# Window attention with a convolutional position term: moving two 64 by 64 matmul stages next to each other, pairing the layer norm's transposes, and reordering the setup and the last block

## The chip, the core and the metric

One NeuronCore of a Trainium2 chip runs the whole program. The metric is device time in microseconds (us) of one execution; the time before is the median of two runs, 5380.8 us (5376.48 and 5385.11). The engines: TensorE (PE in the profile; its weight loads are PEld), VectorE (DVE), ScalarE (ACT), GpSimd (POOL), and SyncE (SP), whose queue here issues nearly all DMAs. PSUM is the memory that TensorE writes; GpSimd has no part in reading it here, so whatever GpSimd adds is first copied to SBUF by ScalarE.

## The reference

```python
# x: (1, 511, 511, 192) bf16; ws = 7, nh = 4, dh = 48
pe = sum over 3x3 taps of shifted x * dw_pe[i, j]      # depthwise convolution
x0 = x + pe
h  = (x0 - mean) / sqrt(var + 1e-5)                    # over the 192 channels
hw = h cut into 73 x 73 windows of 49 tokens
q, k, v = split(hw @ w_qkv)                            # 4 heads of 48
out = softmax(q k^T * 48**-0.5) v @ w_o
return x0 + out                                        # windows put back
```

## The kernel before

**Tiling.** The 5329 windows are cut into 42 blocks: 41 of 128 windows and one of 81. In a block the 128 partitions are windows. `X` (three buffers in turn) holds the block as windows x 49 tokens x 192 channels, `XP` the 9 x 9 patch of every window as 81 partitions x 128 windows x channels, `T` the convolution (with the residual's own tap left to a separate add) as an 81 x 49 matrix for each channel. `HO` (two buffers) holds the normalised tokens channels-first (two halves `kt` of 96 channels); the attention's result is written back into it.

**A group** is 8 windows of a block (16 groups in a block, 11 in the last, 667 in all). Iteration g of the main loop (line 544) issues, in this order on TensorE: q of group g (`stage_A` which=0, line 364); the transposes of the attention result of group g-2 (`stage_E`, 447); k of group g (`stage_A` which=1); the product of probabilities and v of group g-1 (`stage_D`, 423); projections of the block before (`proj`, 459; 13 in a block, 4 tokens each, in groups 2 to 10); one set of layer norm transposes of the next block (`ln_tr`, 343; 7 sets in a block, in groups 10 to 15); the scores (`stage_B`, 402); v (`stage_V`, 380). B and D consist of 32 matmuls each, which use the array as four tiles of 64 by 64 (`tile_position`); all other stages use up to 128 rows and more than 64 columns. `q_`, `k_`, `v_`, `pt` and `o_` are single buffers.

**PSUM.** Every stage takes the next of three two-bank tiles `PS` in turn (`self.PS.next()`), so the fourth stage after one waits until that one's result has been read out. ScalarE reads q, k, v, the exponential of the scores, the projections and the second transpose half; VectorE reads D (a reciprocal and a multiply, lines 432 and 433), the first transpose half, and E in the first groups of a block (ScalarE later, `late`). The convolution has two one-bank tiles `PC`.

**What fills in.** The 192 convolution matmuls of the next block (`conv_mm`, line 298, one per channel, 81 x 128 weights and 49 columns; every ten a VectorE cast into `X`, line 303) are handed out by `fill()` between the long matmuls of `stage_A`, `stage_V` and `proj`, in equal shares for each long matmul, over the first 7 groups of a block. After that `hook(share)`, called at fixed places of an iteration, issues the next block's layer norm in program order: `xs` loads on SP, adds and statistics on VectorE (310, 314), `rstd` and the normalisation on GpSimd (320, 321, 329), then `XP` loads for the block after and the stores on SP. The order on every queue is the program's (`tc.manual_schedule()`); each engine runs its queue in order.

**A transpose set** (`ln_tr`) issues 8 matmuls for `kt` 0, the VectorE copy of that half, 8 matmuls for `kt` 1 and the ScalarE copy, all on one `PS` tile:

```python
            for kt in range(2):
                for i in range(N):
                    mm(pb[0:KT, kt * 1024 + i * 128 : ...], ..., is_transpose=True)
                eng = nc.vector.tensor_copy if kt == 0 else nc.scalar.copy
                eng(out=HO[b % 2][0:KT, kt, :, s0 : s0 + N], in_=pb[0:KT, kt * 1024 : ...])
```

**Setup and ends.** `__init__` clears the buffers, builds `T` in 25 tiles of two tokens (lines 120 and 129), folds the weights and reads a flag that chooses between `fast` and `slow`; `fast` runs. It then loads `XP` of block 0, convolves, normalises and transposes it with nothing beside it (lines 528 to 541), and only then enters the main loop. After the last group, one iteration does all 13 projections of the last block: matmuls, ScalarE copy (`pO`, two buffers), GpSimd add (467), stores on SP.

Of the kernel before, what the change touches and what calls it, by code (L numbers as in the profile page):

```python
# [9 lines left out]
BF = mybir.dt.bfloat16  # L10
# [3 lines left out]
ALU = mybir.AluOpType  # L14
# [47 lines left out]
class _Kernel:  # L62
    def __init__(self, ctx, tc, x, dw_pe, w_qkv, w_o, out, eps, logit_lim):
# [9 lines left out]
        self.PC = _Rot([psum.tile([128, 512], F32, name=f"psc{i}") for i in range(2)])  # L73
        for t in self.PS.t + self.PC.t:
            nc.vector.memset(t[:], 0.0)

        self.ident = consts.tile([128, 128], BF, name="ident")
        make_identity(nc, self.ident[:])
        self.zero = consts.tile([16, C], BF, name="zero")
        nc.vector.memset(self.zero[:], 0.0)  # L80
        self.XP = big.tile([128, BLK, C], BF, name="XP")
        self.XPr = self.XP[0:KP].rearrange("(r q) n c -> q r n c", q=9)
        self.T = big.tile([128, C, S], BF, name="T")
# [4 lines left out]
        gi = consts.tile([1, 1], I32, name="gi")  # L88
        nc.vector.memset(self.XP[:], 0.0)
        for t in self.X:  # L90
            nc.gpsimd.memset(t[:], 0.0)

        with tc.tile_pool(name="setup", bufs=1) as setup:
# [3 lines left out]
            for j in range(3):  # L97
                nc.sync.dma_start(out=dwK[9 * j : 9 * j + 3, :], in_=dw_pe[j])
            for kt in range(2):
# [15 lines left out]
            )  # L115
            for n, s0 in enumerate(range(0, S, 2)):
                ns = min(2, S - s0)
                ps = self.PS.next()
                for ss in range(ns):
                    nc.tensor.matmul(  # L120
                        ps[0:KP, ss * C : (ss + 1) * C],
                        lhsT=Sel[0:21, (s0 + ss) * KP : (s0 + ss + 1) * KP],
                        rhs=dwK[0:21, :],
                        start=True,
                        stop=True,
                    )
                dst = self.T[0:KP, :, s0 : s0 + ns].rearrange("p c s -> p s c")
                src = ps[0:KP, 0 : ns * C].rearrange("p (s c) -> p s c", c=C)
                (nc.vector.tensor_copy if n % 2 == 0 else nc.scalar.copy)(out=dst, in_=src)
# [43 lines left out]
            nc.vector.tensor_copy(out=gi[:], in_=gm[:])  # L173

        cond = nc.values_load(gi[0:1, 0:1], min_val=0, max_val=1)
        with tc.If(cond > 0) as cnd:
            with ExitStack() as c2, tc.manual_schedule():
                self.fast(c2)
        with cnd.Else():
            with ExitStack() as c2:  # L180
                self.slow(c2)


    def fast(self, ctx):
# [38 lines left out]

        def dram(t, h, w, dims):
            return bass.AP(tensor=t.tensor, offset=t.offset + (h * W + w) * C, ap=[list(d) for d in dims])

        zero = self.zero[0:9, :]

        def clear(part, p0, n):

            return lambda: nc.sync.dma_start(
                out=part[:, p0 : p0 + n, :], in_=bass.AP(tensor=zero.tensor, offset=zero.offset, ap=[list(zero.ap[0]), [0, n], [1, C]])
            )

        def load_xp(b):

            for a0, b0, da, db, n, p0 in blocks[b]:
                left = [0] if b0 == 0 else []
                right = [] if b0 + (n - 1) * db < NWC - 1 else list(range(n)) if da else [n - 1]
                if left and any(ln[1] for bb in blocks[:b] for ln in bb):  # L240
                    yield clear(XPr[0], p0, n if da else 1)
                if right and b:
                    yield clear(XPr[8], p0 + right[0], len(right))
                last = a0 + (n - 1) * da
                cuts = [0] + ([1] if da and a0 == 0 else []) + ([n - 1] if da and last == NWR - 1 else []) + [n]
                for i, j in zip(cuts, cuts[1:]):
                    if j <= i:
                        continue
                    top, bot = a0 + i * da == 0, a0 + (j - 1) * da == NWR - 1
                    if top and b:  # L250
                        yield clear(XP[0:9], p0 + i, j - i)
                    if bot and b:
                        yield clear(XP[KP - 9 : KP], p0 + i, j - i)
                    pr0, pr1 = (1 if top else 0), (8 if bot else 9)
                    for pc in range(9):
                        q, sh = (WS - 1, -1) if pc == 0 else (0, 1) if pc == 8 else (pc - 1, 0)
                        n0, n1 = i, j
                        if pc == 0 and left:
                            n0 = j if da else i + 1
                        if pc == 8 and right:  # L260
                            n1 = i if da else j - 1
                        if n1 <= n0:
                            continue
                        dims = [[W * C, pr1 - pr0], [WS * C * (W * da + db), n1 - n0], [1, C]]
                        dst = XPr[pc, pr0:pr1, p0 + n0 : p0 + n1, :]
                        src = dram(x, WS * (a0 + n0 * da) - 1 + pr0, WS * (b0 + n0 * db + sh) + q, dims)
                        yield lambda dst=dst, src=src: nc.sync.dma_start(out=dst, in_=src)

# [56 lines left out]

        def ln_norm(b, s0, s1):
            assert b < 2 or stored.get(b - 2, 0) * 2 * WS >= s1 or stored.get(b - 2, 0) == len(CHUNKS)
            i, n = (49 if s0 == S - 1 else s0), s1 - s0
            nc.gpsimd.tensor_tensor(  # L329
                out=hbuf(b)[:, s0:s1, :],  # L330
                in0=self.X[b % 3][:, s0:s1, :],
                in1=rstd[:, i : i + n].unsqueeze(2).to_broadcast([128, n, C]),
                op=ALU.mult,
            )

        def ln_tr(b, s0, n):
            h = hbuf(b)
            ps = PS.next()
            pb = ps[:].bitcast(BF)
            N = min(8, S - s0)  # L340
            for kt in range(2):
                for i in range(N):
                    mm(  # L343
                        pb[0:KT, kt * 1024 + i * 128 : kt * 1024 + (i + 1) * 128],
                        lhsT=h[:, s0 + i, kt * KT : (kt + 1) * KT],
                        rhs=ident[:],
                        start=True,
                        stop=True,
                        is_transpose=True,
                    )  # L350
                eng = nc.vector.tensor_copy if kt == 0 else nc.scalar.copy
                eng(  # L352
                    out=HO[b % 2][0:KT, kt, :, s0 : s0 + N],
                    in_=pb[0:KT, kt * 1024 : kt * 1024 + N * 128].rearrange("p (s w) -> p w s", w=128),
                )
# [3 lines left out]
        def stage_A(b, ck, which, fill):  # L359
            dst = (q_, k_)[which]  # L360
            ps = PS.next()
            for ab in range(2):
                for kt in range(2):
# [6 lines left out]
                    )  # L370
                    fill()
            nc.scalar.copy(out=dst[:, :, 0:TOK], in_=two_bank(ps, TOK))  # L372

        def stage_V(b, ck, fill, eng):
            ps = PS.next()
            for pi in range(4):
                w = ck * CH + 2 * pi
                col = (pi // 2) * 512 + (pi % 2) * C
                for kt in range(2):
# [6 lines left out]
                    )  # L386
                    fill()
            eng(  # L388
# [83 lines left out]
        def stat_items(b):  # L472
# [54 lines left out]

        xp = list(load_xp(0))
        for t in xp:
            t()  # L530
        n = Next(0)
# [12 lines left out]
        for g in range(NG + LE + 1):  # L544
# [100 lines left out]
    def slow(self, ctx):  # L645
# [22 lines left out]
        for t in (v_, pt):  # L668
            nc.vector.memset(t[:], 1.0)
        mm = nc.tensor.matmul  # L670

        def two_bank(ps, ncol):
# [213 lines left out]
```

## Time and profile before

| | |
|---|---|
| median of two runs | 5380.8 us (5376.48 to 5385.11) |
| the profiled execution | 5363.58 us; its span 5361.9 us |
| mean granted TensorE clock | 0.777 of full |
| PE busy, PE weight loads busy | 4426.2 us (83%), 3610.8 us (67%) |
| ACT, DVE, POOL busy | 3054.3 us (57%), 2727.6 us (51%), 2116.4 us (39%) |
| DMA | 377 MB, mean 70 GB/s |

The span is the time from the first to the last instruction; the profiled execution has 1.7 us around it. [...] Matmuls are pipelined and overlap in the records, so a busy share of PE is not its share of the peak; the waits before instructions and the start of one stage to the start of the next say more.

### The profile page before, as it was taken

The page shows a single profiled execution, that of the slowest core. Times are in us where ns is not written, and L with a number is a line of the kernel's source. Part 1 is how long each engine was busy: PE and PEld are TensorE (multiplying, and loading weights), DVE is VectorE, ACT ScalarE, POOL GpSimd, SP SyncE. Part 2 cuts the span into 40 slices and gives each one's busy share as a digit, 9 for nine tenths or more (in the row PEclk, how much of TensorE's full clock was granted, in tenths as well). Part 3 has the DMA queues.
Part 4 walks back from the last instruction along what each step waited for, and adds up shares of the span by engine and source line. Part 5 has one row for each costly group of instructions (what it writes and reads, how often), then busy time and mean ns, then how long its engine had stood idle before and what let it go on. Part 6 is the DMA issues. An engine that isn't in the chain of part 4 may idle for free. (4 is left out here: it accounts for less than half of the span.)

```text
span 5361.9 us, 167300 instructions
## 1 busy us (share of the span) xinstructions
PE 4426.2 (83%) x75049; PEld 3610.8 (67%) x75049; DVE 2727.6 (51%) x4190; ACT 3054.3 (57%) x3855; POOL 2116.4 (39%) x1188
## 2 busy tenths in 40 slices
PE   2688888888888888888888888888888888888777
PEld 1566776776766666677766766666667776676665
DVE  5554555455555544555545555545554555455542
ACT  1455555556555565556655555555555566555555
POOL 3433333334444433334433444433333343344333
PEclk9886787777777776778877777767777888777777
DMA  2222222233333222222323333222222233233221
GB/s 69 59 68 67 68 68 68 68 78 77 82 80 83 72 68 68 68 68 68 78 68 77 83 80 83 71 67 68 68 68 68 68 78 73 70 74 81 68 48 32
DMA packets 529706, 377.00 MB, mean 70 GB/s; under 512 B 454181, under 2 KB 454373, under 8 KB 528979
## 3 DMA queue, kind: packets, MB, share of 16 engines
q1 hardware_dynamic: 528531, 365.92, 27.9%
q8 instruction: 589, 9.65, 0.8%
q14 instruction: 138, 1.13, 0.1%
q10 hardware_dynamic: 448, 0.30, 0.0%
HBM read 265.31 MB, written 100.27 MB: 68 GB/s over the span
## 5 line engine op out<-in xcount | busy, mean ns | idle before, releaser
L467 POOL TENSOR_TENSOR X<-X,pO 128x768 bf16<-128x768 bf16 (+1 forms) x546 | 894.6, 1654 | 2789.2 <-ACT pO L463 2787.9
L364 PE MATMUL ps<-HO,Wqk 96*128 96x392 bf16 x5336 | 1639.4, 426 | 20.1 <-ACT HO L352 15.8
L298 PEld LDWEIGHTS <-XP 81*128 81x128 bf16 x8064 | 1246.8, 185 | 139.2 <-issue 51.6
L298 PE MATMUL psc<-T,XP 81*128 81x49 bf16 x8064 | 1303.1, 211 | 41.3 <-DMA xs<-in_x_dram 32.0
L380 PE MATMUL ps<-Wv,HO 96*128 96x192 bf16 x5336 | 863.4, 299 | 118.3 <-DVE o L433 112.2
L343 PE MATMUL ps<-ident,X 128*96 128x128 bf16 x4116 | 412.0, 253 | 640.9 <-DVE HO L352 592.0
L432 DVE RECIPROCAL rs<-ps 128x16 f32<-128x16 f32 x667 | 169.8, 255 | 1393.8 <-PE ps L423 896.8
L303 DVE CAST X<-psc 128x490 bf16<-128x490 f32 x840 | 542.8, 646 | 591.5 <-PE psc L298 585.0
L364 PEld LDWEIGHTS <-Wqk 96*128 96x128 bf16 x5336 | 623.7, 124 | 303.8 <-issue 238.1
L352 ACT COPY HO<-ps 96x1024 bf16<-96x1024 bf16 (+1 forms) x294 | 284.5, 968 | 869.7 <-PE ps L343 869.7
L343 PEld LDWEIGHTS <-X 128*96 128x96 bf16 x4116 | 336.8, 148 | 644.7 <-issue 598.6
L372 ACT CAST k<-ps 128x784 bf16<-128x784 f32 x667 | 543.6, 815 | 363.8 <-PE ps L364 269.6
L329 POOL TENSOR_TENSOR X<-X,rstd 128x1536 bf16<-128x1536 bf16 (+1 forms) x294 | 734.2, 2515 | 18.5 <-DMA out_dram<-X 5.4
L380 PEld LDWEIGHTS <-HO 96*128 96x128 bf16 x5336 | 604.6, 122 | 158.6 <-issue 111.7
L459 PE MATMUL ps<-Wo,HO 96*128 96x192 bf16 x4116 | 690.6, 302 | 16.3 <-ACT HO L448 12.7
L388 ACT CAST v<-ps 128x768 bf16<-128x768 f32 x667 | 535.7, 803 | 267.3 <-PE ps L380 218.7
L372 ACT CAST q<-ps 128x784 bf16<-128x784 f32 x667 | 543.7, 815 | 249.2 <-PE ps L364 240.9
L433 DVE TENSOR_TENSOR o<-ps,rs 128x768 bf16<-128x768 f32 x667 | 638.4, 957 | 23.4
L459 PEld LDWEIGHTS <-HO 96*128 96x128 bf16 x4116 | 619.1, 180 | 25.2 <-issue 3.5
L463 ACT CAST pO<-ps 128x768 bf16<-128x768 f32 x504 | 401.4, 799 | 392.3 <-PE ps L459 333.4
L447 PEld LDWEIGHTS <-o 128*96 128x96 bf16 x5336 | 526.4, 166 | 104.5 <-issue 45.8
L410 ACT ACTIVATE pt<-ps 128x784 bf16<-128x784 f32 x667 | 550.8, 826 | 62.6 <-PE ps L402 62.5
(55 smaller groups left out, 4068.3 us busy)
## 6 DMA issues: line engine op xcount, KB each, us to landing
XP<-in_x_dram SPq DMA_DIRECT2D x568, 216.0 KB
xs<-in_x_dram SPq DMA_DIRECT2D x574, 168.0 KB
out_dram<-X SPq DMA_DIRECT2D x246, 336.0 KB
XP<-in_x_dram SPq DMA_DIRECT2D x151, 212.6 KB
out_dram<-X SPq DMA_DIRECT2D x82, 168.0 KB
XP<-in_x_dram SPq DMA_DIRECT2D x16, 192.0 KB
XP<-in_x_dram SPq DMA_DIRECT2D x64, 30.4 KB
xs<-in_x_dram SPq DMA_DIRECT2D x63, 23.6 KB
```

The costliest lines, as they stand in the source:

```text
L298: mm(cv.ps[:, (c % 10) * S : (c % 10 + 1) * S], lhsT=XP[0:KP, :, c], rhs=T[0:KP, c, :], start=True, stop=True)
L303: nc.vector.tensor_copy(out=self.X[cv.b % 3][:, :, c0 : c0 + n], in_=cv.ps[:, 0 : n * S].rearrange("p (c s) -> p s c", s=S))
L329: nc.gpsimd.tensor_tensor(out=hbuf(b)[:, s0:s1, :], in0=self.X[b % 3][:, s0:s1, :], in1=rstd[:, i : i + n].unsqueeze(2).to_broadcast([128, ...
L343: mm(pb[0:KT, kt * 1024 + i * 128 : kt * 1024 + (i + 1) * 128], lhsT=h[:, s0 + i, kt * KT : (kt + 1) * KT], rhs=ident[:], start=True, stop ...
L364: mm(ps[:, ab * 512 : ab * 512 + TOK], lhsT=self.Wqk[kt][0:KT, which * 2 + ab, :], rhs=HO[b % 2][0:KT, kt, ck * CH : (ck + 1) * CH, 0:S], ...
L372: nc.scalar.copy(out=dst[:, :, 0:TOK], in_=two_bank(ps, TOK))
L380: mm(ps[:, col : col + C], lhsT=HO[b % 2][0:KT, kt, w : w + 2, :].rearrange("p w s -> p (w s)"), rhs=self.Wv[kt][0:KT, :], start=(kt == 0) ...
L388: eng(out=v_[:].rearrange("p (b j) h e -> p b (j h) e", b=2)[:, :, :, 0:DH], in_=two_bank(ps, 2 * C).rearrange("p b (g d) -> p b g d", d=DH),)
L410: nc.scalar.activation(out=pt[:, 0 : 16 * S].rearrange("p (b n) -> p b n", b=2), in_=two_bank(ps, 8 * S), func=ACTF.Exp, scale=SCALE)
L433: nc.vector.tensor_tensor(out=o_[:].rearrange("p b q (h d) -> p b (q h) d", d=DH), in0=ov[:, :, :, 0:DH], in1=r_[:].rearrange("p (b g) -> ...
L459: mm(ps[:, col : col + C], lhsT=HO[b % 2][0:KT, kt, :, s0 + i], rhs=self.Wo[kt][0:KT, :], start=(kt == 0), stop=(kt == 1))
L467: nc.gpsimd.tensor_tensor(out=xv, in0=xv, in1=o[:, 0:n, :], op=ALU.add)
```

## The change

- **Adjacent stages.** `stage_D` moves from before the projections and transposes to just before `stage_B`, so that the 64 by 64 stages follow each other.
- **Paired transposes.** `ln_tr` issues all 16 transposes of a set, then the two copies.
- **Convolution.** `proj` calls `fill()` no more; `stage_A` calls it with weight 2 and `stage_V` with weight 1 for each matmul (24 in all).
- **First block.** Three of the seven normalisations of block 0 go to VectorE.
- **Last block.** Seven of the 13 projections of the last block (`direct`) are added by VectorE straight from PSUM, without ScalarE and GpSimd.
- **Setup.** `T` is built in 13 tiles of four tokens, cast with another order of elements; `XP` is cleared first, by VectorE and GpSimd; `X` is cleared last; the `dw_pe` loads go to ScalarE's queue; the loads of `XP` for block 0 (`load_xp`, moved out of `fast` unchanged, with `clear` and `dram`) are issued before the flag is read.

```diff
-        for t in self.PS.t + self.PC.t:
-            nc.vector.memset(t[:], 0.0)
+        self.XP = big.tile([128, BLK, C], BF, name="XP")
+        nc.vector.memset(self.XP[:, 0:88, :], 0.0)
+        nc.gpsimd.memset(self.XP[:, 88:BLK, :], 0.0)
...
-        nc.vector.memset(self.XP[:], 0.0)
-        for t in self.X:
-            nc.gpsimd.memset(t[:], 0.0)
...
-                nc.sync.dma_start(out=dwK[9 * j : 9 * j + 3, :], in_=dw_pe[j])
+                nc.scalar.dma_start(out=dwK[9 * j : 9 * j + 3, :], in_=dw_pe[j])
...
-            for n, s0 in enumerate(range(0, S, 2)):
-                ns = min(2, S - s0)
+            make_identity(nc, self.ident[:])
+            for t in self.PS.t + self.PC.t:
+                nc.vector.memset(t[:], 0.0)
+            for n, s0 in enumerate(range(0, S, 4)):
+                ns = min(4, S - s0)
...
+                if ns == 4:
+                    dst = self.T[0:KP, :, s0 : s0 + ns].rearrange("p c (b s) -> p c b s", b=2)
+                    src = ps[0:KP].rearrange("p (b n) -> p b n", b=2)[:, :, 0 : 2 * C].rearrange("p b (s c) -> p c b s", c=C)
...
+            for t in self.X:
+                nc.gpsimd.memset(t[:], 0.0)
+        for t in self.load_xp(0):
+            t()
         cond = nc.values_load(gi[0:1, 0:1], min_val=0, max_val=1)
...
-        def ln_norm(b, s0, s1):
+        def ln_norm(b, s0, s1, eng=nc.gpsimd):
...
-            nc.gpsimd.tensor_tensor(
+            eng.tensor_tensor(
...
                         is_transpose=True,
                     )
+            for kt in range(2):
                 eng = nc.vector.tensor_copy if kt == 0 else nc.scalar.copy
...
-                    fill()
+                    fill(2)
...
-                    fill()
+                    fill(1)
...
-        def proj(b, s0, fill):
+        def proj(b, s0, direct=False):
...
-                    fill()
+            if direct:
+                for i0 in range(0, n, 2):
+                    m = min(2, n - i0)
+                    xv = self.X[b % 3][:, s0 + i0 : s0 + i0 + m, :]
+                    nc.vector.tensor_tensor(
+                        out=xv, in0=ps[:, i0 * 256 : i0 * 256 + m * C].rearrange("p (s c) -> p s c", c=C), in1=xv, op=ALU.add
+                    )
+                return
...
-                            items.append((2, lambda s0=s0: ln_norm(b, s0, min(S, s0 + 8))))
+                            items.append((2, lambda s0=s0: ln_norm(b, s0, min(S, s0 + 8), nc.vector if b == 0 and s0 % 16 else nc.gpsimd)))
...
-            nlong = 16 + 8 * len(pj)
...
-            def fill():
-                quota[0] += (conv_goal - conv_start) / nlong
+            def fill(weight):
+                quota[0] += (conv_goal - conv_start) * weight / 24
...
-            if 0 <= g - LD < NG:
-                stage_D()
             for s0 in pj:
-                proj(b - 1, s0, fill)
+                proj(b - 1, s0, b == NB and s0 % 8 == 0)
...
             hook(0.55)
             now[0] = g + 0.5
+            if n and g < NG:
+                n.transpose(part(0.56, 0.96, 7), 0.9)
+            if 0 <= g - LD < NG:
+                stage_D()
             if g < NG:
-                if n:
-                    n.transpose(part(0.56, 0.96, 7), 0.9)
                 stage_B()
```

## Rows read from the trace of the kernel before

**Rows 1.** Waits of PE: what for, us in total, times, longest us.
```profile
PE ps L343 <- DVE HO L352: 592.0, 294, 8.8
```

**Rows 2.** Timeline of one late group: start us, us, instructions [idle before <- releaser].
```profile
2621.03 0.61 PE L343 MATMUL ps<-ident,X 128*96 128x128 bf16 x8 [0.23 <-ACT HO L448]
2621.21 0.96 DVE L433 TENSOR_TENSOR o<-ps,rs 128x768 bf16<-128x768 f32 x1
2622.08 1.21 DVE L352 COPY HO<-ps 96x1024 bf16<-96x1024 bf16 x1
2623.34 0.61 PE L343 MATMUL ps<-ident,X 128*96 128x128 bf16 x8 [1.71 <-DVE HO L352]
2623.88 0.44 PE L402 MATMUL ps<-q,k 48*64 48x49 bf16 x32
2624.26 0.83 PE L380 MATMUL ps<-Wv,HO 96*128 96x192 bf16 x8
```

**Rows 3.** Windows, three blocks: stretch, us, busy by engine (count), granted clock, DMA.
```profile
2018.10:2150.60 132.50, 114.91 (x1798) 92.02 (x1797) 63.36 (x99) 72.91 (x92) 49.11 (x28) 0.68 0.28 68
2150.60:2273.40 122.80, 105.06 (x1798) 86.05 (x1797) 64.37 (x99) 72.90 (x92) 49.57 (x28) 0.78 0.30 74
2518.30:2633.10 114.80, 94.00 (x1797) 78.81 (x1797) 63.80 (x99) 71.09 (x92) 49.60 (x28) 0.89 0.32 79
```

**Rows 4.** Windows, three single groups: two with transposes, one that opens a block.
```profile
2618.17:2625.05 6.88, 4.86 (x106) 3.63 (x105) 2.34 (x3) 4.57 (x7) 0.00 (x0) 1.00 0.00 0
2592.01:2601.97 9.96, 7.07 (x106) 5.30 (x104) 6.04 (x11) 4.97 (x7) 7.91 (x3) 0.67 0.75 188
2633.11:2641.39 8.28, 7.59 (x117) 6.06 (x116) 3.13 (x5) 3.42 (x5) 0.00 (x0) 0.50 0.01 3
```

**Rows 5.** Timeline of PE, second transpose half of an earlier group of the block.
```profile
2589.25 1.01 PE L343 MATMUL ps<-ident,X 128*96 128x128 bf16 x8 [3.83 <-DVE HO L352]
```

**Rows 6.** Timeline of PE's weight loads at the entry into D at full clock.
```profile
2620.35 0.34 PEld L423 LDWEIGHTS <-pt 49*64 49x64 bf16 x32 [0.33 <-issue]
```

**Rows 7.** Windows: a projection with and without convolutions, a q stage with and without.
```profile
2553.11:2554.79 1.68, 1.68 (x26) 1.65 (x19) 1.38 (x3) 0.57 (x1) 0.00 (x0) 1.00 0.97 266
2565.24:2566.14 0.90, 0.90 (x17) 0.81 (x9) 0.69 (x2) 0.59 (x1) 0.00 (x0) 1.00 0.91 185
2525.95:2527.03 1.08, 1.08 (x14) 1.07 (x13) 0.49 (x2) 0.80 (x1) 0.00 (x0) 1.00 0.00 0
2562.96:2563.64 0.68, 0.68 (x8) 0.41 (x7) 0.61 (x1) 0.68 (x2) 0.68 (x1) 1.00 0.00 0
```

**Rows 8.** Timeline from the setup to the first group.
```profile
37.66 18.83 DVE L129 CAST T<-ps 81x384 bf16<-81x384 f32 x11 [0.95 <-PE ps L120]
...
59.80 23.48 SPq L267 DMA_DIRECT2D XP<-in_x_dram  x18
...
88.98 17.39 PE L298 MATMUL psc<-T,XP 81*128 81x49 bf16 x192 [32.03 <-DMA xs<-in_x_dram]
...
135.50 0.86 DVE L310 TENSOR_TENSOR X<-X,xs 128x1344 bf16<-128x1344 bf16 x1 [23.29 <-DMA xs<-in_x_dram]
...
140.33 6.07 POOL L329 TENSOR_TENSOR X<-X,rstd 128x1536 bf16<-128x1536 bf16 x2
140.52 3.27 DVE L310 TENSOR_TENSOR X<-X,xs 128x1344 bf16<-128x1344 bf16 x1
...
165.44 0.51 POOL L329 TENSOR_TENSOR X<-X,rstd 128x192 bf16<-128x192 bf16 x1
...
171.08 0.53 PE L364 MATMUL ps<-HO,Wqk 96*128 96x392 bf16 x1
```

**Rows 9.** Timeline of the end.
```profile
5332.35 9.15 PE L459 MATMUL ps<-Wo,HO 96*128 96x192 bf16 x64 [0.74 <-DVE HO L448]
...
5334.84 19.82 POOL L467 TENSOR_TENSOR X<-X,pO 128x768 bf16<-128x768 bf16 x13 [20.69 <-ACT pO L463]
...
5341.39 18.18 SPq L283 DMA_DIRECT2D out_dram<-X  x36
```

More of the change, by code (lines that the diff above doesn't have):

```diff
@@ L73, in __init__ @@
         self.PC = _Rot([psum.tile([128, 512], F32, name=f"psc{i}") for i in range(2)])
-        for t in self.PS.t + self.PC.t:
-            nc.vector.memset(t[:], 0.0)
+        self.XP = big.tile([128, BLK, C], BF, name="XP")
+        self.XPr = self.XP[0:KP].rearrange("(r q) n c -> q r n c", q=9)
+        nc.vector.memset(self.XP[:, 0:88, :], 0.0)
+        nc.gpsimd.memset(self.XP[:, 88:BLK, :], 0.0)
         self.ident = consts.tile([128, 128], BF, name="ident")
-        make_identity(nc, self.ident[:])
         self.zero = consts.tile([16, C], BF, name="zero")
         nc.vector.memset(self.zero[:], 0.0)
-        self.XP = big.tile([128, BLK, C], BF, name="XP")
-        self.XPr = self.XP[0:KP].rearrange("(r q) n c -> q r n c", q=9)
         self.T = big.tile([128, C, S], BF, name="T")
@@ L120, in __init__ @@
                     nc.tensor.matmul(
-                        ps[0:KP, ss * C : (ss + 1) * C],
+                        ps[0:KP, (ss // 2) * 512 + (ss % 2) * C : (ss // 2) * 512 + (ss % 2 + 1) * C],
                         lhsT=Sel[0:21, (s0 + ss) * KP : (s0 + ss + 1) * KP],
@@ L126, in __init__ @@
                     )
-                dst = self.T[0:KP, :, s0 : s0 + ns].rearrange("p c s -> p s c")
-                src = ps[0:KP, 0 : ns * C].rearrange("p (s c) -> p s c", c=C)
+                if ns == 4:
+                    dst = self.T[0:KP, :, s0 : s0 + ns].rearrange("p c (b s) -> p c b s", b=2)
+                    src = ps[0:KP].rearrange("p (b n) -> p b n", b=2)[:, :, 0 : 2 * C].rearrange("p b (s c) -> p c b s", c=C)
+                else:
+                    dst = self.T[0:KP, :, s0 : s0 + ns]
+                    src = ps[0:KP, 0 : ns * C].rearrange("p (s c) -> p c s", c=C)
                 (nc.vector.tensor_copy if n % 2 == 0 else nc.scalar.copy)(out=dst, in_=src)
@@ L181, in __init__, with dram, clear, load_xp @@
                 self.slow(c2)
+    def dram(self, t, h, w, dims):
+        return bass.AP(tensor=t.tensor, offset=t.offset + (h * self.W + w) * C, ap=[list(d) for d in dims])
+    def clear(self, part, p0, n):
+        nc, zero = self.nc, self.zero[0:9, :]
+        return lambda: nc.sync.dma_start(
+            out=part[:, p0 : p0 + n, :], in_=bass.AP(tensor=zero.tensor, offset=zero.offset, ap=[list(zero.ap[0]), [0, n], [1, C]])
+        )
+    def load_xp(self, b):
+        nc, x, XP, XPr, W, NWR, NWC = self.nc, self.x, self.XP, self.XPr, self.W, self.NWR, self.NWC
+        blocks, clear, dram = _blocks(NWR, NWC), self.clear, self.dram
+        for a0, b0, da, db, n, p0 in blocks[b]:
+            left = [0] if b0 == 0 else []
+            right = [] if b0 + (n - 1) * db < NWC - 1 else list(range(n)) if da else [n - 1]
+            if left and any(ln[1] for bb in blocks[:b] for ln in bb):
+                yield clear(XPr[0], p0, n if da else 1)
+            if right and b:
+                yield clear(XPr[8], p0 + right[0], len(right))
+            last = a0 + (n - 1) * da
+            cuts = [0] + ([1] if da and a0 == 0 else []) + ([n - 1] if da and last == NWR - 1 else []) + [n]
+            for i, j in zip(cuts, cuts[1:]):
+                if j <= i:
+                    continue
+                top, bot = a0 + i * da == 0, a0 + (j - 1) * da == NWR - 1
+                if top and b:
+                    yield clear(XP[0:9], p0 + i, j - i)
+                if bot and b:
+                    yield clear(XP[KP - 9 : KP], p0 + i, j - i)
+                pr0, pr1 = (1 if top else 0), (8 if bot else 9)
+                for pc in range(9):
+                    q, sh = (WS - 1, -1) if pc == 0 else (0, 1) if pc == 8 else (pc - 1, 0)
+                    n0, n1 = i, j
+                    if pc == 0 and left:
+                        n0 = j if da else i + 1
+                    if pc == 8 and right:
+                        n1 = i if da else j - 1
+                    if n1 <= n0:
+                        continue
+                    dims = [[W * C, pr1 - pr0], [WS * C * (W * da + db), n1 - n0], [1, C]]
+                    dst = XPr[pc, pr0:pr1, p0 + n0 : p0 + n1, :]
+                    src = dram(x, WS * (a0 + n0 * da) - 1 + pr0, WS * (b0 + n0 * db + sh) + q, dims)
+                    yield lambda dst=dst, src=src: nc.sync.dma_start(out=dst, in_=src)
@@ L221, in two_bank @@
             return ps[:].rearrange("p (b n) -> p b n", b=2)[:, :, 0:ncol]
[L224 to L267, printed above, removed]
@@ L269, in strips @@
+        dram, load_xp = self.dram, self.load_xp
         def strips(b, r0, r1):
@@ L459, in proj @@
                     mm(ps[:, col : col + C], lhsT=HO[b % 2][0:KT, kt, :, s0 + i], rhs=self.Wo[kt][0:KT, :], start=(kt == 0), stop=(kt == 1))
-                    fill()
+            if direct:
[4 more added lines that the diff above has]
+                        out=xv, in0=ps[:, i0 * 256 : i0 * 256 + m * C].rearrange("p (s c) -> p s c", c=C), in1=xv, op=ALU.add
+                    )
+                return
             o = pO.next()
@@ L526, in transpose @@
                 return False
-        xp = list(load_xp(0))
-        for t in xp:
-            t()
         n = Next(0)
@@ L670, in slow @@
         mm = nc.tensor.matmul
+        nc.vector.memset(XP[:], 0.0)
         def two_bank(ps, ncol):
```

## The prediction

> **What bounds the kernel now.** The page says PE 83% busy, no other engine above 57%, so I read first what PE waits for. One wait is over half of PE's idle time: the transposes on line 343 wait for VectorE's copy on line 352, 592.0 us in 294 waits [rows 1]. 294 is 42 blocks times 7 sets: each set waits once, 2.01 us (592.0 / 294). The timeline shows the mechanism [rows 2]: eight transposes at 2621.03; VectorE is still multiplying D's result (2621.21), copies the first half from 2622.08 for 1.21 us; only then, at 2623.34, do the other eight transposes start, after 1.71 us of idling, although they fill the other half of the tile. Where the statistics of the next block also stand in VectorE's queue, the wait is longer [rows 5].
>
> Second, the granted clock. Three whole blocks do the same work (the counts agree) in 132.5, 122.8 and 114.8 us at 0.68, 0.78 and 0.89 of the clock [rows 3]. So one hundredth of clock is worth (132.5 - 114.8) / 21 = 0.84 us in a block, while busy DVE, ACT and POOL times hardly move: PE sets the pace, and its clock sets PE's. Within the groups with transposes the clock is 1.00 in one and 0.67 in another [rows 4].
>
> **Paired transposes.** PE's wait goes: with all 16 matmuls ahead of both copies there is no copy for PE to wait for inside a set. 7 x 2.01 = 14.1 us in a block. What is late next: D, B and V follow and take the next PSUM tiles, and V's tile is the one the transposes used. The VectorE copy ends about 0.1 + 1.21 us after the last transpose; D and B cover 2 x 0.38 us at full clock (B's start to V's start, [rows 2]), so V waits some 0.55 us; at the lower clock D and B last about twice as long and cover it. I take 0.35 us for four sets, 0.4 for the short last one, and 1.0 us for the two sets behind statistics: their 3.83 us [rows 5] is covered by the other eight transposes, D and B for only about half. Together 1.4 + 0.4 + 2.0 = 3.8 us return, and the gain is 10.3 us x 41 = **420 us**. Bounds: nothing returns (578), twice as much returns (266).
>
> **Clock.** PE's longest regular idling disappears, so I expect it at the lower level less often. No row shows the changed kernel's clock; the nearest are the blocks at 0.78 and 0.89 [rows 3], alike but for how often the clock fell. I take halfway, 0.835: 5.5 x 0.84 = 4.6 us in a block, 41 blocks, **190 us**; bounds 0 and 380.
>
> **D next to B.** D's 32 matmuls, a reciprocal and a multiply are moved behind the projections, hook(0.55) and the transposes; D issues no DMA. On VectorE its two instructions now stand behind that hook's adds and statistics and behind the transpose copy. Who waits for that: E of the next iteration, which has B, V and q to cover it, and q's PSUM tile. In the groups with statistics V waits for D's result now and q will instead; I count this as even. What is saved is one change into 64 by 64 tiles (P or transposes to B) in some 13 groups of 16. At the entry into D the weight load idles 0.33 us [rows 6], but most of that lies under matmuls still running. Bounds: 0 and 0.33 x 13 x 41 = 176 us; I take 0.08 us each, near the lower end because the matmul rows show hardly a gap, **40 us**. B's wait for k does not grow: projections or transposes still stand between k and B.
>
> **Convolutions out of the projections.** A projection with 9 of them takes 1.68 us, without 0.90: 87 ns each; q with 7 takes 1.08, without 0.68: 57 ns each [rows 7]. By the old equal shares about 59 of 192 sit in projections (three groups with 16 of 32 shares, two with 8 of 24, 27.4 a group). 59 x 0.030 x 41 = 72 us; I take **60**, since the new shares put nine convolutions in q and k, more than those rows have. Bounds 0 and 72. VectorE's casts keep their number.
>
> **Setup and first block.** The first convolution starts 29.2 us after the first XP load is issued (88.98 - 59.80, [rows 8]). The loads now pass SP's wait for the flag and start after the two halves of XP's clearing, some 9 us by my estimate: 38 us. But VectorE's clears at the head of the main part come before the first cast, and T must be ready: 11 casts take 18.83 us now; 13 casts of twice the size take between less than that and twice as long on two engines. Start of convolution between 38 and 70 us; I take 47, gain 42. `dw_pe` on ScalarE's queue and X's clearing at the end of GpSimd's setup have cover, the XP loads. Behind that, the chain to the first group (xs loads, queued behind block 1's XP loads, at 135.50) only shifts. The seven first sets lose their waits, and GpSimd's last normalisation comes earlier: 10 us more, **52 us** in all (25 to 65). A row warns of the shared normalisation: VectorE's add of two SBUF operands at 140.52 took 3.27 us beside GpSimd's normalisation, and 0.86 at 135.50 alone [rows 8]; three normalisations on VectorE may take turns with GpSimd's and not run beside them. [...]
>
> **Last block.** GpSimd's 13 adds take 19.82 us [rows 9]; shared they'd take about half. But the 36 stores occupy SP for 18.18 us from 5341.39, nine for each quarter of the tokens, and they end last. They can start some 4 us earlier and pack closer: **7 us** (3 to 10).
>
> **Sum.** 420 + 190 + 40 + 60 + 52 + 7 = 769 us off the profiled execution's 5363.6 us gives 4595; it lies 17 us under the median of the runs, so 4612, rounded to **4610 us**.
>
> **Rivals.**
> *The wait comes back at V.* If the ScalarE half is read only after VectorE's (1.21 + 1.01 us, as the order was), or both sit behind other work, V waits 0.1 + 2.2 - 0.76 = 1.55 us in each set, and 1 us more in two: 12.9 of the 14.1 us return, and the clock gains nothing. For: V's tile is the transposes' tile, three stages on. Against: the copies are on two engines and read different banks. 5363.6 - 49 - 159 (the four small terms) + 17 = 5172. Chance 0.12.
>
> *The wait isn't removed at all*, because something other than the copy of the first half holds the second: only the four small terms, 5222 us. Against: the second half starts right behind the copy's end [rows 2]. Chance 0.03.
>
> *The clock falls: slower.* [...] The place is the last six groups of a block and those that follow: a block opens at 0.50 and needs 8.28 us for its first group although PE is busy 7.59 of it [rows 4]. If the clock then stays at 0.50 all through, it costs 0.28 x 84 x 41 = 960 us against 4802 (the sum without its clock term): 5760 us. It decides from a mean clock of 0.61 down: there (5381 - 4802) / (84 x 41) = 0.17 of clock is lost and the gain is gone; at 0.575 the kernel is 2% slower. Against: a group with 16 transposes and a wait ran at 1.00 throughout [rows 4]. Chance 0.05. [...]
>
> **How the numbers follow.** Forecast 0.80, at 4610 us. Its range: down 190 us for the clock of the fastest block, and half of what the returning waits and the switches could still give (80 + 60), 4300 rounded up a little; up 190 us for a clock that stays and 130 for waits and shares that return nearly to their bounds: 4930. The rivals lie outside, 0.20 in all, so this is the range. Two per cent is about what a measurement of this kernel tells from no change. Forecast and most of the first two rivals are faster by more: 0.93. Their upper edges and a part of the clock's rival lie within 2%: 0.04. A clock under 0.575: 0.03.
>
> **What would show it.** Transposes waiting for the copy of their own set: gone. V waiting for line 352: some 0.5 us, 200 times or more. Mean clock 0.83 or so; below 0.78 the clock term is wrong, below 0.61 the forecast. Blocks of about 107 us (122.8 - 10.3 - 4.6 and 1 to 2 for switches and convolutions). Projections of 0.9 us wherever they stand. First convolution near 47 us, first group near 119. GpSimd's normalisations may become what transposes wait for when groups shorten; that would lift the late groups over 7 us and the time towards the upper end.

## The result: 5380.8 to 4794.4 us, and the profile after

The changed kernel takes 4794.35 us (two runs, 4794.18 and 4794.51), 0.891 of the kernel before [0.8872, 0.8948]. Forecast: 4610, range 4300 to 4930. The span shrank from 5361.9 to 4792.8 us, 569 us; 769 were expected. The mean granted clock rose from 0.777 to 0.863, more than the 0.835 expected.

The waits of PE after (what for, us, times, longest us) answer to [rows 1]:

```profile
PE ps L391 <- ACT HO L363: 395.5, 246, 6.2
PE ps L413 <- ACT pO L483: 107.6, 38, 3.8
PE ps L391 <- ACT pO L481: 90.2, 318, 1.1
PE ps L375 <- DVE o L444: 76.2, 46, 1.9
PE ps L353 <- POOL X L339: 48.2, 3, 38.5
```

The transposes (now line 353) wait no more for the copy of their own set. V (391) does instead, and for ScalarE's copy, not VectorE's: 395.5 us in 246 waits, 1.61 us each; 246 is six of a block's seven sets, 41 times. Two waits are new with D's new place: V and the scores (413) wait for copies of projections, 90.2 and 107.6 us. One late group at full clock, in the timeline (start us, us, instructions, [idle before <- releaser]), which answers to [rows 2], and then the row of the page for ScalarE's copy (busy us, mean ns | idle before, releaser):

```profile
2307.86 1.06 PE L353 MATMUL ps<-ident,X 128*96 128x128 bf16 x16
2308.85 0.44 PE L434 MATMUL ps<-v,pt 49*64 49x49 bf16 x32
2309.03 1.22 DVE L363 COPY HO<-ps 96x1024 bf16<-96x1024 bf16 x1 [1.66 <-ACT k L383]
2310.28 1.01 ACT L363 COPY HO<-ps 96x1024 bf16<-96x1024 bf16 x1 [1.35 <-DVE HO L363]
2311.34 0.82 PE L391 MATMUL ps<-Wv,HO 96*128 96x192 bf16 x8 [1.79 <-ACT HO L363]
```

```profile
L363 ACT COPY HO<-ps 96x1024 bf16<-96x1024 bf16 (+1 forms) x294 | 284.2, 967 | 413.6 <-DVE HO L363 411.3
```

ScalarE stood idle for 1.35 us and began at 2310.28, when VectorE's copy ended, although its half had been in PSUM since 2308.92. The two copies run one after the other: 1.22 + 1.01 us, less what D and B cover, leaves V 1.79 us. Over the kernel ScalarE's copy waits 411.3 us for VectorE's.

Windows (stretch, us, busy and count of PE, PEld, DVE, ACT, POOL, granted clock, DMA share, GB/s): two blocks answer to [rows 3], the group above to the first of [rows 4], then q with nine convolutions, k with none and a projection to [rows 7], then all 41 whole blocks, after and (last row) before:

```profile
2224.90:2332.70 107.80, 89.66 (x1797) 77.89 (x1797) 63.60 (x99) 72.35 (x93) 48.90 (x28) 0.90 0.34 84
2115.50:2224.90 109.40, 90.94 (x1797) 78.77 (x1797) 63.76 (x99) 72.61 (x93) 48.89 (x28) 0.89 0.33 83
...
2307.86:2313.82 5.96, 4.17 (x106) 3.53 (x105) 2.81 (x4) 4.11 (x6) 5.88 (x3) 1.00 0.69 166
...
2249.93:2251.20 1.27, 1.27 (x16) 1.27 (x15) 0.67 (x1) 0.80 (x1) 0.62 (x1) 1.00 0.00 0
2270.45:2271.14 0.69, 0.69 (x8) 0.47 (x6) 0.42 (x1) 0.61 (x1) 0.34 (x1) 1.00 0.85 187
2271.14:2271.97 0.83, 0.83 (x9) 0.74 (x8) 0.16 (x1) 0.58 (x1) 0.00 (x0) 1.00 1.02 201
...
130.14:4701.56 4571.42, 3789.31 (x73491) 3266.39 (x73491) 2617.51 (x4055) 2963.66 (x3761) 1982.64 (x1135) 0.86 0.32 79
171.08:5267.70 5096.62, 4316.39 (x73491) 3520.11 (x73491) 2615.11 (x4055) 2968.07 (x3760) 2003.02 (x1135) 0.77 0.29 71
```

These 41 blocks give 525 of the 569 us: 124.3 to 111.5 us a block. To split these 12.8 us, take two blocks at the same clock. At 0.89 a block took 114.80 [rows 3] and takes 109.40: **5.4 us** come from less work and waiting at equal clock, and the other **7.4** from the clock (8.6 hundredths at the prediction's 0.84 us are 7.2). That is one pair of blocks; the averages over the 41 say nearly the same: from 0.77 to 0.86 of the clock, 9 hundredths are 7.6 us, which leaves 5.2.

Setup to first group, timeline, against [rows 8]:

```profile
15.76 1.10 DVE L131 CAST T<-ps 81x768 bf16<-81x768 f32 x1 [1.34 <-PE ps L118]
...
36.02 1.99 PE L308 MATMUL psc<-T,XP 81*128 81x49 bf16 x20 [5.92 <-DMA XP<-in_x_dram]
...
44.79 15.56 PE L308 MATMUL psc<-T,XP 81*128 81x49 bf16 x172 [6.79 <-DVE X L313]
...
89.62 0.86 DVE L320 TENSOR_TENSOR X<-X,xs 128x1344 bf16<-128x1344 bf16 x1 [23.42 <-DMA xs<-in_x_dram]
...
94.41 1.76 DVE L339 TENSOR_TENSOR X<-X,rstd 128x1536 bf16<-128x1536 bf16 x1 [3.33 <-POOL rstd L331]
94.45 4.32 POOL L339 TENSOR_TENSOR X<-X,rstd 128x1536 bf16<-128x1536 bf16 x1
...
103.36 0.21 POOL L330 TENSOR_SCALAR tmp<-bnst 128x16 f32<-128x16 f32 x1 [4.59 <-DVE bnst L324]
...
130.14 0.34 PE L375 MATMUL ps<-HO,Wqk 96*128 96x392 bf16 x1 [1.86 <-DVE HO L363]
```

The first group starts at 130.14, 40.9 us earlier than at 171.08. The convolution starts at 36.02, stops after 20 matmuls because VectorE's clears stand ahead of its first cast, and goes on at 44.79. The end, against [rows 9]:

```profile
4768.47 10.72 PE L470 MATMUL ps<-Wo,HO 96*128 96x192 bf16 x98 [0.74 <-DVE HO L459]
...
4775.76 14.79 SPq L293 DMA_DIRECT2D out_dram<-X  x36
```

From the last projections to the end of the span it is 24.3 us; it was 29.5 (5361.9 - 5332.35).

### The profile page after: what moved, and what is told of

It is laid out like the page before. It is cut to its first block, busy times and chain, and to the rows that moved or that the text cites. A ratio compares the mean times of both kernels' runs of the same rounds, so it can differ in the third digit from the quotient of the medians.

```text
span 4792.8 us, 167033 instructions
## 1 busy us (share of the span) xinstructions
PE 3893.8 (81%) x75049; PEld 3356.2 (70%) x75049; DVE 2722.9 (57%) x4200; ACT 3029.9 (63%) x3842; POOL 2087.7 (44%) x1179
## 4 chain that ended last, share of the span: by engine, by line
PE 56%; ACT 13%; DVE 11%; POOL 8%; issue 4%; SPq 4%; DMA 3%; ACTq 0%; DVEq 0%; POOLq 0%
PE ps L375 20%; PE ps L391 11%; PE psc L308 9%; PE ps L458 7%; ACT pO L481 6%; DVE HO L363 5%; POOL X L339 5%; ACT HO L363 5%; PE ps L353 4%; PE ps L470 4%; SPq L234 3%; DVE bnst L324 3%; DMA XP<-in_x_dram 3%; DVE X L320 2%; POOL X L485 2%
## 5 line engine op out<-in xcount | busy, mean ns | idle before, releaser
L485 POOL TENSOR_TENSOR X<-X,pO 128x768 bf16<-128x768 bf16 (+1 forms) x539 | 859.5, 1610 | 2322.9 <-ACT pO L481 2321.2
L375 PE MATMUL ps<-HO,Wqk 96*128 96x392 bf16 x5336 | 1632.4, 397 | 113.7 <-DVE o L444 76.2
L308 PEld LDWEIGHTS <-XP 81*128 81x128 bf16 x8064 | 1101.5, 177 | 164.9 <-issue 105.7
L391 PE MATMUL ps<-Wv,HO 96*128 96x192 bf16 x5336 | 718.0, 267 | 485.9 <-ACT HO L363 395.5
L308 PE MATMUL psc<-T,XP 81*128 81x49 bf16 x8064 | 1080.2, 221 | 37.4 <-DMA XP<-in_x_dram 28.2
L375 PEld LDWEIGHTS <-Wqk 96*128 96x128 bf16 x5336 | 656.0, 127 | 321.3 <-issue 211.2
L391 PEld LDWEIGHTS <-HO 96*128 96x128 bf16 x5336 | 556.4, 109 | 450.2 <-issue 419.0
L363 DVE COPY HO<-ps 96x1024 bf16<-96x1024 bf16 (+1 forms) x294 | 336.9, 1147 | 784.9 <-ACT k L383 402.5
L363 ACT COPY HO<-ps 96x1024 bf16<-96x1024 bf16 (+1 forms) x294 | 284.2, 967 | 413.6 <-DVE HO L363 411.3
L324 DVE BATCH_NORM_STATS2 bnst<-X 128x6 f32<-128x384 bf16 x1050 | 528.0, 549 | 10.1
L458 PE MATMUL ps<-ident,o 128*96 128x128 bf16 x5336 | 527.4, 256 | 1.4 <-DVE o L444 1.4
L470 PE MATMUL ps<-Wo,HO 96*128 96x192 bf16 x4116 | 461.4, 263 | 1.0 <-DVE HO L459 0.7
L470 PEld LDWEIGHTS <-HO 96*128 96x128 bf16 x4116 | 441.5, 183 | 25.8 <-issue 14.6
```

The costliest lines, as they stand in the source:

```text
L308: mm(cv.ps[:, (c % 10) * S : (c % 10 + 1) * S], lhsT=XP[0:KP, :, c], rhs=T[0:KP, c, :], start=True, stop=True)
L324: nc.vector.bn_stats(out=bnst[:, i, :], in_=self.X[b % 3][:, s : s + 2, :].rearrange("p s c -> p c s"))
L375: mm(ps[:, ab * 512 : ab * 512 + TOK], lhsT=self.Wqk[kt][0:KT, which * 2 + ab, :], rhs=HO[b % 2][0:KT, kt, ck * CH : (ck + 1) * CH, 0:S], ...
L391: mm(ps[:, col : col + C], lhsT=HO[b % 2][0:KT, kt, w : w + 2, :].rearrange("p w s -> p (w s)"), rhs=self.Wv[kt][0:KT, :], start=(kt == 0) ...
L458: mm(ev, lhsT=o_[:, sl, Q, kt * KT : (kt + 1) * KT], rhs=ident[:], start=True, stop=True, is_transpose=True)
L485: nc.gpsimd.tensor_tensor(out=xv, in0=xv, in1=o[:, 0:n, :], op=ALU.add)
```

## The experiments

Ratios are against the kernel before on the same chip (median 5360.4 for the first four, 5365.1 for the rest). The 5380.8 above is from another measurement, so ratios from there and from here are compared, not times.

**pair_only: the pairing alone, on the kernel before.**

```diff
+            for kt in range(2):
                 eng = nc.vector.tensor_copy if kt == 0 else nc.scalar.copy
```

> The kernel before with one edit: all 16 transposes of a set are issued ahead of its two copies; D stays ahead of the projections. Theory 'the pairing brings the gain, and gives part back': the 592 us wait inside the sets goes; the transposes' PSUM tile is next taken by q of the next group instead of V, so some 1.5 us a set (41 x 7) come back in front of q, and the clock rises to about 0.83: 5000 us, 4900 to 5100. Rival 'the neighbouring 64 by 64 stages bring a large part' (one array switch fewer in 13 of 16 groups): 5200 or more here.

4944.57 us, 0.9241 [0.9206, 0.9277], within what was expected. The longest wait, and one block in the windows:

```profile
PE ps L365 <- ACT HO L353: 279.3, 239, 2.3
```

```profile
2540.00:2648.90 108.90, 92.55 (x1796) 77.38 (x1796) 65.34 (x99) 70.78 (x93) 49.62 (x28) 0.91 0.33 83
```

The wait moved here too: with D still ahead of the transposes, the stage that takes the transposes' tile next is q of the next group, and it waits 1.17 us, not V's 1.61. The block at 0.91 stands for 110.6 us at 0.89 (2 x 0.84 more), against 114.80: 4.2 us a block or 172 of the 416 us at equal clock. By this pair of blocks more than half is the clock, 0.844 here.

**adj_only: D moved to just before B, on the kernel before.**

```diff
-            if 0 <= g - LD < NG:
-                stage_D()
             for s0 in pj:
...
+            if n and g < NG:
+                n.transpose(part(0.56, 0.96, 7), 0.9)
+            if 0 <= g - LD < NG:
+                stage_D()
```

> The kernel before with one edit: D is issued just before B. Theory 'the pairing brings the gain': the wait inside the transpose sets stays, a little shorter because D's multiply no longer stands ahead of the transpose copy; projections' tiles are taken again by V two stages later and V waits some 0.35 us for them, against 0.1 us less for the array switch: between 5250 and 5420 us. Rival 'the neighbouring stages bring a large part': 5150 us or less.

4934.44 us, 0.9204 [0.9174, 0.9235]: as much as the pairing, where I expected almost nothing. The theory missed, and the rival's number held. The wait, a set at full clock in the timeline, and one block in the windows:

```profile
PE ps L343 <- DVE HO L352: 508.2, 294, 8.8
```

```profile
2647.65 1.22 DVE L352 COPY HO<-ps 96x1024 bf16<-96x1024 bf16 x1 [4.18 <-PE ps L343]
2648.92 0.61 PE L343 MATMUL ps<-ident,X 128*96 128x128 bf16 x8 [1.38 <-DVE HO L352]
```

```profile
2546.30:2659.20 112.90, 92.28 (x1797) 79.75 (x1797) 64.75 (x99) 72.98 (x92) 49.08 (x28) 0.88 0.32 80
```

D's multiply no longer stands ahead of the copy in VectorE's queue: VectorE is idle when the transposes end, and the second half waits 1.38 us where it waited 1.71 [rows 2]. The block at 0.88 is only about 2.7 us below what [rows 3] give for that clock (114.80 + 0.84); by this pair the rest of its 10.3 us a block is the clock, at 0.858. Waiting didn't become less: PE's idle time is 997.9 us here (span 4939.5 less 3941.6 busy) and was 935.7 (5361.9 - 4426.2). All of this gain is shorter busy time of the same matmuls.

**noadj: the changed kernel with D back ahead of the projections.**

```diff
+            if 0 <= g - LD < NG:
+                stage_D()
             for s0 in pj:
...
-            if 0 <= g - LD < NG:
-                stage_D()
```

> The changed kernel with one part undone: D goes back ahead of the projections and transposes. Theory 'next to each other costs more than it saves': V's wait for the projection's copy (0.35 us in some 9 groups a block, against 0.1 us for the array switch) goes, and the wait for the transposes' tile moves one stage later, to q (1.5 instead of 1.8 us): 4620 us, 4550 to 4720. Rival 'the neighbouring stages bring a gain': above 4830 us.

4911.05 us, 0.9178 [0.9142, 0.9214]. A miss: it was expected below the changed kernel, and the rival's number held. The move is worth 2.7 points here too (0.9178 against 0.891). The wait for ScalarE's copy shrank, from 395.5 us, but did not go, and V waits for D:

```profile
PE ps L375 <- ACT HO L363: 260.0, 207, 2.2
PE ps L391 <- DVE o L444: 133.3, 107, 2.9
```

**pc: the changed kernel, each transpose half on a PSUM tile of its own** (the convolution's two one-bank tiles, which are free by then).

```diff
-            ps = PS.next()
-            pb = ps[:].bitcast(BF)
+            pb = [PCB.next()[:].bitcast(BF) for _ in range(2)]
```

> The changed kernel with one edit: the two halves of a transpose set go to the convolution's two one-bank PSUM tiles, idle at that point of a block, instead of to one two-bank tile. Theory 'two readers of one PSUM tile take turns': ScalarE's copy no longer waits for VectorE's (411 us before it now), and V doesn't wait for either (395 us now): 4350 us, 4280 to 4450, mean clock above 0.88. Rival 'the late groups are bound by ScalarE, VectorE or GpSimd': the wait shows elsewhere (D's result, the normalisations), 4650 us or more.

4559.35 us, 0.8496 [0.846, 0.8532]: between the two numbers, and outside both. The wait named is gone, and another came. That wait, and a set in the timeline:

```profile
PE ps L374 <- DVE o L443: 300.4, 219, 5.8
```

```profile
2301.80 3.38 DVE L320 TENSOR_TENSOR X<-X,xs 128x1344 bf16<-128x1344 bf16 x1
...
2302.61 1.06 PE L352 MATMUL psc<-ident,X 128*96 128x128 bf16 x16
2303.84 1.03 ACT L362 COPY HO<-psc 96x1024 bf16<-96x1024 bf16 x1
2304.40 0.83 PE L390 MATMUL ps<-Wv,HO 96*128 96x192 bf16 x8
...
2306.61 1.20 DVE L362 COPY HO<-psc 96x1024 bf16<-96x1024 bf16 x1
...
2308.01 0.96 DVE L443 TENSOR_TENSOR o<-ps,rs 128x768 bf16<-128x768 f32 x1
2309.02 1.34 PE L374 MATMUL ps<-HO,Wqk 96*128 96x392 bf16 x4 [3.79 <-DVE o L443]
```

ScalarE's copy runs at 2303.84, 2.8 us **before** VectorE's. So what held it was neither the engine nor the data but the shared tile: with a tile for each half there is no order between the readers. What is late next stands here as well: VectorE does an add and three statistics, then the transposes' copy, and only then D's multiply; q, which takes D's tile, waits 3.79 us for it. The prediction had that wait and called it even. In the changed kernel that holds (76.2 us at q, where V waited 112.2 before), but not here. One thing `pc` doesn't separate: with it the transposes also leave the three `PS` tiles, so V's tile is no longer theirs. How much of the 4 points comes from the order of the readers alone is open.

**defer: the kernel before, with D's matmuls where they were, and only its two VectorE instructions issued behind the transposes' first copy** (in the groups with transposes). TensorE's order is unchanged; no 64 by 64 stages are neighbours.

```diff
-                stage_D()
+                read = stage_D()
+                if ck < 10:
+                    read()
...
+            if 0 <= g - LD < NG and ck >= 10:
+                read()
```

> The kernel before with one edit, on VectorE's queue alone: in groups 10 to 15 of a block D's matmuls stay where they were, but D's reciprocal and multiply are issued behind the transposes' first copy. TensorE's order, and so every change between 128-row and 64 by 64 stages, is that of the kernel before. Theory 'moving D helped by freeing VectorE's queue ahead of the transpose copy': most of what moving D alone gave (0.92 of before) comes here too, 5000 us, 4930 to 5120, with V now waiting a little for D's multiply. Rival 'neighbouring 64 by 64 stages save array switches': 5250 us or more.

5068.24 us, 0.9446 [0.9407, 0.9485]: inside the expected range, and 5.5 of the 8.0 points of adj_only without any neighbouring stages. So some two thirds of what the move gives can be had from VectorE's order alone:

```profile
PE ps L343 <- DVE HO L352: 424.4, 294, 8.8
PE ps L380 <- DVE o L436: 136.3, 181, 2.8
```

What gives the last 2.5 points was not separated: the adjacency itself, or D's tile, whose late reading now holds V (136.3 us in 181 waits; 112.2 in 43 in the kernel before).

**pc_noadj: pc with D back ahead**, both edits above.

> The changed kernel with the transposes on the convolution's two PSUM tiles and with D back ahead of projections and transposes. Theory 'what counts is which tile and which queue the waits run through, not the neighbourhood of D and B': q's wait for D's multiply (300 us with the transposes on those tiles and D late) goes, no wait of its size takes its place: 4300 us, 4230 to 4420. Rival 'neighbouring stages are worth 100 us or more': 4600 or more.

4438.27 us, 0.8273 [0.8238, 0.8309], 138 us above the forecast and 18 above its range: a miss, though the side was right and it is the fastest of all. A wait did take the place of q's, 166.5 us at V. That wait, and a set in the timeline:

```profile
PE ps L390 <- DVE o L443: 166.5, 114, 7.2
```

```profile
2321.34 1.09 PE L352 MATMUL psc<-ident,X 128*96 128x128 bf16 x16
2321.83 0.96 DVE L443 TENSOR_TENSOR o<-ps,rs 128x768 bf16<-128x768 f32 x1
...
2322.47 1.01 ACT L362 COPY HO<-psc 96x1024 bf16<-96x1024 bf16 x1 [0.24 <-PE psc L352]
2322.71 1.21 DVE L362 COPY HO<-psc 96x1024 bf16<-96x1024 bf16 x1
2322.74 0.83 PE L390 MATMUL ps<-Wv,HO 96*128 96x192 bf16 x8
```

D's multiply is done under the transposes, the copies run side by side, and V starts without waiting. They take 1.01 and 1.21 us here, side by side on two tiles, and 1.01 and 1.22 one after the other in the changed kernel (2310.28 and 2309.03). The move of D, worth 8 points while the copy on VectorE held the transposes, costs 2.2 points (0.8273 against 0.8496) once V waits for neither copy.

**oldfill: the changed kernel with the convolutions back in the projections**, in the old equal shares.

```diff
-                    fill(2)
+                    fill()
...
-                    fill(1)
+                    fill()
...
+                    fill()          # in proj
```

> The changed kernel with the old shares of the convolution (equal for each long matmul, projections included). By the prediction's term (87 ns for one in a projection, 57 in q) it is 60 us slower than the changed kernel: 0.902 of before. By the groups of the profile that run at full clock in both (5.84 and 6.03 us, 6.58 and 6.63) the new shares give nothing: 0.885 to 0.894 of before.

4802.78 us, 0.8953 [0.8926, 0.8981]. The changed kernel itself was not timed on this chip; noends below, which is within 4 us of it by its parts, gave 4794.67. So the shares are worth some 8 us by that, and some 23 by the ratios (0.8953 against 0.891, whose intervals overlap): not 60, and not clear of nothing.

**noends: the changed kernel with all normalisations of block 0 on GpSimd, and all of the last block's projections through ScalarE and GpSimd.**

```diff
-    ln_norm(b, s0, min(S, s0 + 8), nc.vector if b == 0 and s0 % 16 else nc.gpsimd)
+    ln_norm(b, s0, min(S, s0 + 8), nc.gpsimd)
...
-                proj(b - 1, s0, b == NB and s0 % 8 == 0)
+                proj(b - 1, s0, False)
```

> The changed kernel with all normalisations of block 0 on GpSimd again and all projections of the last block by way of ScalarE and GpSimd again. [...] Shared projections: the time from the last q to the end (33.4 us) is longer by 5.

4794.67 us, one run. The two parts go opposite ways, and the first goes against the prediction, which had GpSimd's last normalisation come earlier with VectorE's help. The first group, in the timeline:

```profile
94.10 6.07 POOL L339 TENSOR_TENSOR X<-X,rstd 128x1536 bf16<-128x1536 bf16 x2
94.29 3.27 DVE L320 TENSOR_TENSOR X<-X,xs 128x1344 bf16<-128x1344 bf16 x1
...
122.20 0.51 PE L375 MATMUL ps<-HO,Wqk 96*128 96x392 bf16 x1 [1.80 <-DVE HO L363]
```

It starts at 122.20, 7.9 us **earlier** than with VectorE's help, and the stretch from the last q to the end takes 4.5 us longer (37.9 against 33.4).

## Why the prediction was right, and where it wasn't

The side and the range were right. The forecast is 184 us off, and the terms are further off than their sum:

| term | predicted | measured |
|---|---|---|
| paired transposes | 420 | 197 (592.0 - 395.5 us of waits) |
| clock | 190 | 304 (7.4 x 41) |
| D next to B, convolutions | 40 + 60 | 24 together (5.4 x 41 - 197) |
| setup and first block | 52 | 41 |
| last block | 7 | 5 |

The right column adds up to 571, of 569; its second and third rows split what is left over, and are good to some tens of us. The rows say where the time shows, not what an edit gives: the pairing alone gave 416 us (`pair_only`), and D's move 2.7 points on top of it (`noadj`), each with the clock that it brings. Nor is the 197 a net gain: the two new waits of the third row, 90.2 + 107.6 us, are as long, and PE's idle time as a whole fell only from 935.7 to 899.0 us (4792.8 - 3893.8).

**Paired transposes: mis-sized.** The wait inside the set goes as said, 14.1 us a block, but 9.6 return at V (395.5 / 41), not 3.8. V is the third stage after the transposes, and with three tiles the third stage waits (not the fourth, as "PSUM" above has it). The step that failed is "V waits some 0.55 us": it let both copies run at once, since they are on two engines and read different banks. The program orders the two readers of one tile: ScalarE's copy waits 411.3 us for VectorE's, and in `pc`, with a tile each, it ran 2.8 us ahead of VectorE's in the set shown (2303.84 and 2306.61). By the group at 2307.86 V would have waited some 0.7 us without that order (an estimate: 2309.55, when V is ready, to 2310.25, the end of VectorE's copy), near the 0.55 forecast; it waited 1.79. That is the first rival's mechanism. It priced a set at 1.55 us, and 1 us more behind statistics, 12.9 in a block; 1.61 came on the mean of six, 9.6 in a block. That rival was given 0.12, and the sign that spoke for it, "as the order was", stood in the kernel before: both copies read one `PS` tile. Its second half, that the clock then gains nothing, is what failed there, and so its 5172 us. The lower clock doesn't cover V's wait as forecast: at 0.50 B's start to V's takes 0.57 us in the kernel before (2138.52 to 2139.09), 1.5 times the 0.38 at full clock and not about twice, and two of them cover 1.14 of the 1.31 us.

**Clock: mis-sized, low.** I tied the clock to the wait that goes and took halfway. It rose from 0.777 to 0.863 although two thirds of the waiting came back, and in `pair_only` and `adj_only`, with 279 and 508 us of the wait left, to 0.844 and 0.858. The clock rose with each change of the late groups (to 0.815 in `defer`), and by the pairs of blocks above more than half of each gain is clock. The step that failed is the tie to that wait: in `adj_only` the clock rose about as far with 508 of its 592 us left, and PE's total idle time hardly fell in the changed kernel and rose in `adj_only`. That less idling raises the clock was a guess of mine; what raised it these runs don't tell. The "lower level" is 0.50: of 190 windows of half a microsecond from 2018 to 2113 us of the kernel before, 120 read 0.50, 64 read 1.00, and six a value between.

**D next to B: the wrong mechanism.** The move was priced as array changes saved at 0.08 us each, an estimate that no run shows by itself, and the shift on VectorE as even. On the old kernel it is worth 426 us by itself, and some two thirds of that come from the order on VectorE's queue (`defer`): D's multiply stood ahead of the copy that the transposes waited for, and [rows 2] shows that (2621.21 to 2622.17, the copy after it). The way from that order to the time is not shown, since the wait fell by only 84 us (to 508.2) in `adj_only` and 168 (to 424.4) in `defer`, of 426 and 297 gained, and the rest goes with the clock. Those rows were read for the wait and not for what stood ahead of its releaser. In the changed kernel the pairing has already taken part of that wait, so the two gains overlap: 7.6 and 8.0 points alone, 10.9 together. In groups with projections V waits for the projection's copy instead (90.2 us in 318 waits), and B for the one-token one (107.6 us).

**Convolutions: nothing to speak of.** Averages were compared (87 ns each in a projection, 57 in q with seven) where the next one seems to decide. q takes 1.27 us with nine, 0.58 more than the 0.69 without; seven cost 0.40 [rows 7]. The two added cost 0.18, 90 ns each, by one pair of stages: as much as in the projection they came from. Projections did fall to 0.83 us, as expected (0.9).

**Setup.** The first convolution came at 36.02 and most of them from 44.79; 47 was forecast. The first group came at 130.14, not 119. The chain behind only shifts, as said: 46.5 us from there to the first added `xs` before, 44.8 after. The shared normalisation lost instead of helping: no run shows the part of the sum's 10 us that stands for it, and without it the first group starts 7.9 us earlier (`noends`). First the row: VectorE's 1.76 us beside GpSimd's 4.32, where GpSimd alone takes 2.73 (5.46 us for two, in the blocks that follow), and VectorE's next add takes 2.47 at 97.01 where it takes 0.84 alone, so they largely take turns. But the loss comes from what is queued behind: VectorE also makes the statistics, and GpSimd's next step waits 4.59 us for them (103.36), where the same step in `noends` doesn't wait. The step that failed is "GpSimd's last normalisation comes earlier": it starts 35.0 us after the first add of `xs` (124.62 - 89.62), and 29.9 in `noends` (119.20 - 89.27).

**Last block.** 5.2 us for the 7 forecast, of which `noends` gives 4.5 to the shared adds. The stores still end last, and pack closer (14.79 us for 36, before 18.18 [rows 9]).

**The rivals.** The wait that isn't removed: no such wait is left. The clock that falls: a group with 16 transposes in a row ran at 1.00 (5.96 us, above), and the mean rose. In that group the transposes are 1.06 of the 5.96 us; no run here shows what the transposes do to the clock.

**The signs.** Blocks of 107 us came only at a clock of 0.90; GpSimd's normalisation did not become the bound of the blocks (48.2 us in 3 waits, all but 1.2 before the first group).

## What to carry to other kernels

Where two engines each read half of a PSUM tile, look in the trace whether the second reader waits for the first (411.3 us here) before you price them as parallel; if it does, try a tile for each half. When a wait is found, read what stands in its releaser's queue ahead of it; a stage far off on the waiting engine may be the one to move, and the best place changes once the wait is gone. Price work that is moved between stages by what the next instruction costs there, not by the average of those that are there already. And compare stretches at the same granted clock: a wait that is gone need not be the gain.

## What was not expected of the chip

- A PSUM to SBUF cast of 768 elements into `T` takes 1.10 us with the new order of elements; with the old one a cast of 384 came every 1.71 us (18.83 / 11, [rows 8]).
- The add of 1344 elements on VectorE takes 0.84 to 0.86 us alone (101.38 and 89.62 in the changed kernel), and up to 3.38 beside a GpSimd normalisation (2301.80 in `pc`).
- In `pc_noadj`, blocks go from 97.40 us at 0.95 of the clock to 123.10 at 0.72 near the end of the run, with equal work. In the three blocks from 3868 to 4235 us PE waits for patch loads, for 26.4 us (two blocks in the windows, then the wait in that stretch):

```profile
2237.10:2334.50 97.40, 87.78 (x1797) 74.86 (x1796) 63.98 (x99) 70.21 (x93) 50.17 (x28) 0.95 0.38 93
3984.70:4107.80 123.10, 105.61 (x1797) 86.02 (x1796) 63.83 (x99) 71.33 (x93) 49.10 (x28) 0.72 0.30 72
```

```profile
PE psc L308 <- DMA XP<-in_x_dram: 26.4, 3, 9.7
```

That is a part of what these blocks lose: the middle one alone takes 25.7 us more. Why the loads come late and the clock falls there was not tried; it is what to look at next.
